# Two edits to the load order of a fused attention and feed-forward kernel: eight attention loads behind a feed-forward step, and one weight load cut in two

## The chip, the core and the metric

The kernel runs on one core of a Trainium2 chip. The core has a matrix engine (TensorE; PE in the profile, with PEld for its weight loads), VectorE (DVE), ScalarE (ACT), GpSimd (POOL) and a sync engine (SP), and 16 DMA engines that they share. Each engine works through its own list of instructions in order and waits on semaphores for the others. The metric is the device time of one execution in microseconds (us), and the median of several runs is compared.

## What is computed

Sliding-window causal attention over 8 sequences of 576 tokens with 8 heads of 64, then a gated feed-forward block (SwiGLU) over the 4608 tokens. Inputs are float32; the kernel works in bf16 on the chip and writes float32.

```python
scores = q @ k.T / 8
mask = (rel >= 0) & (rel < 64)          # rel = query position - key position
attn = softmax(where(mask, scores, -1e9))
x = (attn @ v) reshaped to [4608, 512]  # heads side by side
g = x @ w_gate                          # [512, 1536]
out = (silu(g) * (x @ w_val)) @ w_out   # [1536, 512]
```

## The kernel before, in words

**Tiles.** The 4608 tokens are 36 chunks of 128 (number n) and 9 groups of 512 (c). Chunk n belongs to group n // 4. For the attention a chunk needs its own keys and the last 64 of the chunk before, so the work for chunk n reads k and v of n - 1 and n. The 1536 columns of the feed-forward block are 12 slices of 128 (f).

**Steps.** `F(c, fs, lo, hi)` computes slices fs of group c for the tokens lo to hi of the group: 4 gate products per slice on PE into one PSUM bank, a tanh on ACT (tile sig), 4 value products into a second bank, then two operations on DVE (tiles uu and hT). Its products are recorded on line 918, and it keeps the last of them as `self.lastF`. `O`, `O2` and `O3` are the output products of 128 tokens (12 matmuls on line 962), their copy (to tile ost) and, for O and O3, the store. `S2(n)` is the scores of chunks n and n + 1 (PE lines 471 and 475), their exponentials on ACT (line 483) and a mask multiplication on DVE (line 497). `AVw(n)` is the weighted values of chunks n and n + 1 (PE line 620, chunk n first and then n + 1) and their division by the row sums on DVE. `B2(n)` does the scores of chunks n + 2 and n + 3 interleaved with the weighted values of n and n + 1. `X(n)` transposes the attention result xb of chunk n into xT, which F reads. Up to chunk 5 this is done on PE, and from chunk 6 on by a DMA transpose on SP's queue (line 808).

**Loads.** All loads of k, q, v and weights are DMAs issued by POOL, which casts float32 to bf16 on the way. They go out in the order of the program and share one software queue (q0 in the profile). Keys and queries of chunks 4 to 11 come in pairs of chunks through `load2` (tiles ks and qs, line 335) and are transposed on PE by `T64` (line 385). From chunk 12 on they come one chunk at a time through `load` (tiles kn and qn, line 325) and are transposed by DMA on SP (`Tkq`, `T`, line 370). SP's queue is in order: X(6), X(7), then the four transposes of chunks 12 and 13, then X(8), X(9), and so on. `load` and `load2` take a gate: a DMA with a gate is issued only after the operation named, and all that stands behind it on POOL waits with it.

**The order around the change.** It is written out by hand in `build`. In the opening, POOL issues k and q of chunks 2 and 3, v of chunks 0 to 3, the weights of slices 0 to 3 with four copies between them, the weights of slices 4 to 7, k and q of chunks 4 and 5, the weights 8 to 11, and so on up to `halves(4)` and `halves(5)`: two copies on POOL each, which put the halves of two value tiles side by side in tile vs (line 256). AVw(4) reads them, the first two for chunk 4 and the last two for chunk 5. Group 0's F steps run on PE meanwhile, with T64(2) between F(0, (6,)) and F(0, (7,)).

Then group 1 starts. Its first 256 tokens (chunks 4 and 5) are ready first, so F is done on the halves: F(1, fs, 0, 256) for the slices 0 to 11 two at a time, and then F(1, fs, 256, 512), which needs xT of chunks 6 and 7. From AVw(6) on the order is: AVw(6), X(6), X(7), T64(4), O(0, 1), F(1, (6, 7), 0, 256), F(1, (8, 9), 0, 256), S2(8), T64(5), the transposes of chunks 12 and 13, F(1, (10, 11), 0, 256), F(1, (0, 1), 256, 512), O2(0, 2), B2(8), X(8), X(9), F(1, (2, 3), 256, 512), a gated load of k and q of chunks 14 and 15, F(1, (4, 5), 256, 512), O2(0, 3) and B2(10). B2(10) is the first to read k and q of chunks 12 and 13 and v of chunks 10 and 11 (the tiles va 0 and 1).

**PSUM banks.** There are eight; each step takes the one that was used longest ago in the order of the program. F(1, (2, 3), 256, 512) takes the bank from which DVE has copied O2(0, 2), and the second scores of B2(8) take the bank of the value products of F(1, (0, 1), 256, 512), which DVE reads last.

**Semaphores of DMAs.** POOL's DMAs use 16 semaphores in turn, so each also waits for the one 16 before it.

Of the kernel before, what the change touches and what calls it, by code (L numbers as in the profile page):

```python
# [153 lines left out]
class _Kernel:  # L154
# [218 lines left out]
    def T64(self, st):  # L373
# [4 lines left out]
        def pe(e):  # L378
            for i, (x, src, _) in enumerate(loads):
                for a in range(8):  # L380
                    for u in range(2):
                        r = slice(64 * u, 64 * u + 64)
                        for p in range(2):
                            o = bx[u][0].bitcast(BF)[64 * p:64 * p + 64, 512 * i + 64 * a:512 * i + 64 * a + 64]
                            z = e.transpose(o, src[r, a, p, :], self.ident[r, r])  # L385
            return z
# [539 lines left out]
    def F(self, c, fs, lo=0, hi=512, mid=None, side=False):  # L926
        do = self.Fp(c, fs, lo, hi, side)
        for a in range(len(fs)):
            do("Wg", a)
        if mid:  # L930
            mid()
        do("tan", 0)
        for a in range(len(fs)):
            do("Wv", a)
        do("end", 0)

    def O(self, c, u, mid=None):
        io = (4 * c + u) % self.NO
        self.Omm(c, u, 0, 512, "act", [("ost", io), ("osth", io)], mid=mid)
        self.store(c, u)  # L940
# [56 lines left out]
    def loads(self):  # L997
        self.first_loads()
        self.init()
        self.init_mask()  # L1000
        done = self.init_nmask()
        self.init_va(2, 4)
        for i in range(4):
            self.zero(self.vs[i][:, :, 64:80], [("vs", i, 0), ("vs", i, 1)], 1.0)
        self.load2(1, done)
        for n in range(4):
            self.load(n, "v")
        self.W(0, 2)
        self.shift(0, 1, "pool")
        self.W(2, 4)  # L1010
        self.shift(2, 0, "pool")
        self.shift(2, 1, "pool")
        self.shift(3, 0, "pool")
        self.load_w("g", 4, 8)
        self.load_w("v", 4, 6)
        self.load_w("v", 6, 8)

    def early_loads(self):
        self.load2(2)
# [18 lines left out]

    def next_loads(self):
        self.load2(5)  # L1040
        for n in (12, 13):
            self.load(n, "kq")
        for n in (10, 11):
            self.load(n, "v")

    def loop_loads(self, n):
        for m in (n + 6, n + 7):
# [8 lines left out]
    def build(self):  # L1056
# [96 lines left out]
            ev("q", u, "act")  # L1153
        O(0, 1)
        F(1, (6, 7), 0, 256)
        F(1, (8, 9), 0, 256)
        self.init_kmask()
        self.S2(8)
# [34 lines left out]
        for c in range(2, NFC):  # L1193
            for u in range(4):
                n = 4 * c + u + 4
# [6 lines left out]
                v = u + 1 if c == 2 else u  # L1202
# [71 lines left out]
```

## Time and profile before

| What | us |
|---|---|
| Runs before | 326.47, 327.15, 329.30; median 327.15 |
| The profiled execution, whole | 327.38 |
| Its span in the profile | 325.6 |
| PE busy | 318.3 |
| DVE busy | 220.0 |
| ACT busy | 125.7 |
| POOL busy | 106.0 |

The span starts at the first instruction and ends at the last. All times in the rows below are microseconds from its start. The whole execution is 1.78 us longer than the span; that part lies around it. The granted clock of PE is 1.00 in this execution.

The profile also shows the DMA engines in 40 equal slices of 8.14 us each, as a share of all 16 that is busy, in tenths:

```profile
DMA  7999999969999989959999997999687312000012
```

From 8 to 65 us the slices stand at 9. Three queues share the engines:

```profile
q0 software_dynamic: 99504, 18.36, 69.6%
q1 hardware_dynamic: 42864, 10.89, 23.8%
q10 hardware_dynamic: 5472, 9.83, 8.8%
```

Each row is a queue with its packets, the megabytes written and the share of 16 engines' span. q0 holds the DMAs that POOL issues, q1 those of SP (the transposes, and the first loads), q10 those of ACT (the stores of the output).

A row of the timeline gives the start, the length, the engine, the line, the operation and its tiles, and in brackets how long the engine had been idle and what released it. "Landing" is the time from the issue of a DMA to its completion.

### The profile page before, as it was taken

What the parts mean: (1) busy time and instruction counts of PE and PEld (TensorE: products, weight loads), DVE (VectorE), ACT (ScalarE), POOL (GpSimd) and SP (SyncE); (2) the same over time, 40 slices, a digit from 0 to 9 for tenths busy, and PEclk for the clock granted to TensorE, in tenths of its full rate; (3) what the DMA queues carried; (4) which work ended last, traced back from release to release, by engine and by line L of the source; (5) the groups of instructions that cost most, each with busy time, mean ns of one, the idle gap of its engine ahead of it and who ended that gap; (6) DMA issues with size and microseconds to landing.
All of it is one profiled execution on the core that took longest, in us unless ns stands there. A gap on an engine that the chain in (4) does not pass through costs nothing.

```text
span 325.6 us, 8051 instructions
## 1 busy us (share of the span) xinstructions
PE 318.3 (98%) x3446; PEld 169.3 (52%) x3446; DVE 220.0 (68%) x408; ACT 125.7 (39%) x226; POOL 106.0 (33%) x137
## 2 busy tenths in 40 slices
PE   7999999799999999999999999999999999999996
PEld 5655677568544554545444454545454544444444
DVE  6788996679485966675858585858676767555510
ACT  3834565634332543333324242424242422322311
POOL 6999790041726051607060606151402000000000
DMA  7999999969999989959999997999687312000012
GB/s 188 178 199 188 200 183 188 143 93 139 153 165 153 133 86 142 162 117 142 132 104 125 141 151 73 139 131 158 84 102 106 74 34 64 34 32 32 34 64 97
DMA packets 147875, 39.59 MB, mean 122 GB/s; under 512 B 131328, under 2 KB 142848, under 8 KB 147840
## 3 DMA queue, kind: packets, MB, share of 16 engines
q0 software_dynamic: 99504, 18.36, 69.6%
q1 hardware_dynamic: 42864, 10.89, 23.8%
q10 hardware_dynamic: 5472, 9.83, 8.8%
q8 instruction: 27, 0.44, 0.6%
q14 instruction: 8, 0.07, 0.1%
HBM read 37.75 MB, written 9.44 MB: 145 GB/s over the span
## 4 chain that ended last, share of the span: by engine, by line
PE 91%; DMA 4%; POOL 2%; issue 1%; DVE 1%; ACT 1%
PE ps L918 55%; PE ps L962 29%; DMA Wv<-in_moe_w_val_dram 3%; PE ps L729 2%; DMA va<-in_v_dram 2%; PE ps L521 2%; PE ps L471 1%; PE ps L385 1%; POOL vs L256 1%; PE ps L475 0%; POOL va L325 0%; PE ps L620 0%; ACT xT L255 0%; POOL ks L335 0%; PE ps L552 0%
## 5 line engine op out<-in xcount | busy, mean ns | idle before, releaser
L918 PE MATMUL ps<-xT,Wg 128*128 128x512 bf16 (+1 forms) x496 | 111.2, 352 | 1.7 <-issue 1.7
L904 DVE SCALAR_TENSOR_TENSOR uu<-sig,ps 128x512 bf16<-128x512 bf16 x108 | 73.9, 684 | 56.0 <-ACT sig L899 55.6
L918 PE MATMUL ps<-xT,Wv 128*128 128x512 bf16 (+1 forms) x496 | 111.0, 352 | 0.3 <-DMA Wv<-in_moe_w_val_dram 0.3
L899 ACT ACTIVATE sig<-ps 128x512 bf16<-128x512 f32 x108 | 65.1, 602 | 89.4 <-PE ps L918 89.4
L962 PE MATMUL ps<-Wo,hT 128*128 128x512 bf16 (+1 forms) x444 | 98.7, 373 | 0.0
L906 DVE SCALAR_TENSOR_TENSOR hT<-uu,ps 128x512 bf16<-128x512 bf16 x108 | 74.2, 687 | 3.8
L918 PEld LDWEIGHTS ps<-xT,Wv 128*128 128x128 bf16 x496 | 48.3, 98 | 45.4 <-DVE uu L904 0.8
L918 PEld LDWEIGHTS ps<-xT,Wg 128*128 128x128 bf16 x496 | 46.7, 98 | 44.5 <-issue 2.1
L962 PEld LDWEIGHTS ps<-Wo,hT 128*128 128x128 bf16 x444 | 43.3, 98 | 49.0
L325 POOL DMA_DIRECT2D kn<-in_k_dram x27 | 23.0, 853 | 113.9 <-PE ps L918 113.9
L325 POOL DMA_DIRECT2D va<-in_v_dram x40 | 34.2, 878 | 24.9 <-PE ps L918 24.9
L255 ACT ACTIVATE ost<-ps 128x512 f32<-128x512 f32 (+1 forms) x22 | 12.9, 588 | 53.2 <-PE ps L962 53.2
L256 DVE COPY ost<-ps 128x512 f32<-128x512 f32 (+1 forms) x15 | 10.1, 674 | 30.6 <-PE ps L962 30.6
L531 ACT ACTIVATE pt<-ps 128x512 bf16<-128x512 f32 x36 | 18.6, 602 | 29.0 <-PE ps L521 29.0
L325 POOL DMA_DIRECT2D qn<-in_q_dram x27 | 23.1, 861 | 0.0
L483 ACT ACTIVATE pt<-ps 128x512 bf16<-128x512 f32 x28 | 14.5, 602 | 14.7 <-PE ps L475 14.7
L764 DVE TENSOR_TENSOR xb<-ps,rc 128x512 bf16<-128x512 f32 (+2 forms) x39 | 18.8, 509 | 0.5
L729 PE MATMUL ps<-va,pt 64*64 64x65 bf16 x800 | 12.3, 192 | 0.0
L497 DVE TENSOR_TENSOR pt<-pt,kmask 128x1024 bf16<-128x1024 bf16 x18 | 11.5, 682 | 0.0
L729 PEld LDWEIGHTS ps<-va,pt 64*64 64x64 bf16 x800 | 10.4, 107 | 0.0
L497 DVE TENSOR_TENSOR pt<-pt,mask 128x1024 bf16<-128x1024 bf16 x14 | 9.3, 689 | 1.2 <-ACT pt L483 1.1
L760 DVE RECIPROCAL rc<-ps 128x8 f32<-128x8 f32 (+2 forms) x39 | 5.7, 173 | 6.4 <-PE ps L729 6.4
(76 smaller groups left out, 142.2 us busy)
## 6 DMA issues: line engine op xcount, KB each, us to landing
out_dram<-ost ACTq DMA_DIRECT2D x35, 256.0 KB, 2.6
va<-in_v_dram POOLq DMA_DIRECT2D x32, 128.0 KB, 5.8
kn<-in_k_dram POOLq DMA_DIRECT2D x21, 128.0 KB, 4.4
qn<-in_q_dram POOLq DMA_DIRECT2D x21, 128.0 KB, 4.6
Wv<-in_moe_w_val_dram POOLq DMA_DIRECT2D x6, 256.0 KB, 9.2
Wo<-in_moe_w_out_dram POOLq DMA_DIRECT2D x4, 384.0 KB, 14.4
Wg<-in_moe_w_gate_dram POOLq DMA_DIRECT2D x4, 256.0 KB, 8.5
ks<-in_k_dram POOLq DMA_DIRECT2D x3, 256.0 KB, 10.8
```

The lines of the kernel that those rows point to most:

```text
L256: return self.g.op(eng, lambda e: e.tensor_copy(d, a), reads=reads, writes=writes, after=after)
L325: self.g.op("pool", lambda e, d=d, a=a: e.dma_start(d, a), writes=ks, dma=True, after=gate)
L483: g.op("act", lambda e, po=po, p=p: e.activation(po, sv[p], ACTF.Exp, scale=SCALE), reads=[bx[p][1]], writes=[pk[p]])
L497: self.g.op("dve", lambda e: e.tensor_tensor(pt, pt, m, ALU.mult), reads=pk + mk, writes=pk)
L531: g.op("act", lambda e, po=po, p=p: e.activation(po, sv[p], ACTF.Exp, scale=SCALE), reads=[bx[p][1]], writes=[pk[p]])
L729: x = e.matmul(o, ab[0], ab[1], start=first, stop=phase == 1, skip_group_check=True)
L764: g.op("dve", lambda e, av=av, hs=hs, w=w, rc=rc, xo=xo: e.tensor_tensor(xo[:, :, hs, :], av[:, :, :, 0:64], rc[:, :, hs].unsqueeze(3).to_ ...
L899: g.op("act", lambda e: e.activation(sig[:, 0:w], G[:, 0:w], ACTF.Tanh, scale=0.5), reads=[gk], writes=[("sig", i)])
L904: g.op("dve", lambda e: e.scalar_tensor_tensor(uu[:, 0:w], sig[:, 0:w], 1.0, G[:, 0:w], ALU.add, ALU.mult), reads=[("sig", i), gk], writes ...
L906: g.op("dve", lambda e: e.scalar_tensor_tensor(out, v3(uu), 0.5, v3(V), ALU.mult, ALU.mult), reads=[("uu", i), vk], writes=[("hT", ih, f, ...
L918: r = e.matmul(bank[:, a * n:a * n + n], W[:, kk, f * 128:f * 128 + 128], xT[:, kk, lo:hi], start=(kk == 0), stop=(kk == NK - 1))
L962: r = e.matmul(OB[:, 0:n], hT[:, f, 128 * u:128 * u + 128], self.Wo[:, f, lo:hi], start=(f == 0), stop=(f == NF - 1))
```

## The change

Two edits:

1. The weights of slices 4 to 7 were loaded as one DMA of the gate weights for four slices and two DMAs of the value weights for two slices each. Now there are four DMAs of two slices each, in the order gate 4 and 5, value 4 and 5, gate 6 and 7, value 6 and 7. `W(a, b)` issues a gate load and a value load.
2. The loads of k and q of chunks 12 and 13 (six DMAs, since chunk 13 crosses from one sequence to the next) and of v of chunks 10 and 11 (two DMAs) stood right behind `load2(5)` with no gate. Now they stand behind F(1, (6, 7), 0, 256) and wait for its last product.

```diff
@@ loads @@
-        self.load_w("g", 4, 8)
-        self.load_w("v", 4, 6)
-        self.load_w("v", 6, 8)
+        self.W(4, 6)
+        self.W(6, 8)
@@ next_loads @@
     def next_loads(self):
         self.load2(5)
+
+    def after_loads(self):
         for n in (12, 13):
-            self.load(n, "kq")
+            self.load(n, "kq", self.lastF)
         for n in (10, 11):
-            self.load(n, "v")
+            self.load(n, "v", self.lastF)
@@ build @@
         F(1, (6, 7), 0, 256)
+        self.after_loads()
         F(1, (8, 9), 0, 256)
```

The instructions of PE, DVE, ACT and SP keep their order; POOL has one DMA more.

## The prediction

> **What bounds the kernel now.** I read the busy shares first, then PE's waits, then the timeline around each wait.
>
> ```profile
> PE 318.3 (98%) x3446; PEld 169.3 (52%) x3446; DVE 220.0 (68%) x408; ACT 125.7 (39%) x226; POOL 106.0 (33%) x137
> ...
> PE ps L918 <- issue: 1.7, 1, 1.7
> ```
>
> PE is busy for 98% of the span, so the load order can act only through PE's few stalls. This wait is the longest. It is called "issue": the profile shows no releaser. The timeline around it, and around a wait on a weight DMA:
>
> ```profile
> 21.71 1.03 PE L918 MATMUL ps<-xT,Wv 128*128 128x512 bf16 x4
> 22.57 1.03 PE L918 MATMUL ps<-xT,Wg 128*128 128x512 bf16 x4
> 23.93 1.02 PE L918 MATMUL ps<-xT,Wv 128*128 128x512 bf16 x4 [0.34 <-DMA Wv<-in_moe_w_val_dram]
> ...
> 57.72 1.05 PE L918 MATMUL ps<-xT,Wg 128*128 128x256 bf16 x8
> 58.60 1.04 PE L918 MATMUL ps<-xT,Wv 128*128 128x256 bf16 x8
> 61.34 1.03 PE L918 MATMUL ps<-xT,Wg 128*128 128x256 bf16 x8 [1.69 <-issue]
> ```
>
> A step of four such products takes 0.86 from start to start (22.57 - 21.71), one of eight halves 0.88. So PE was ready at 23.43 and began at 23.93 (0.50 lost), and was ready at 59.48 and began at 61.34 (1.86 lost). The last row is F(1, (0, 1), 256, 512), the first reader of X(6) and X(7).
>
> ```profile
> 51.40 2.64 SPq L808 DMA_TRANSPOSE xT<-xb  x2
> ...
> xT<-xb SPq DMA_TRANSPOSE x1, 8.5
> ...
> q0 software_dynamic: 4000, 0.57, 187.7%
> q10 hardware_dynamic: 144, 0.26, 17.8%
> ...
> xT<-xb SPq DMA_TRANSPOSE x1, 2.4
> ```
>
> SP issues X(6) and X(7) at 51.40 and about 52.7. X(7) took 8.5 to land, at 61.2: that is the stall, 0.1 before PE's start. The two queue rows are for the stretch 51.4 to 55.8: the load queue q0 moved 4000 packets, and the transposes' queue q1 has no row. The last line is X(8), issued at 68.02 with no load on the way: 2.4.
>
> **The loads leave the transposes' way.**
>
> ```profile
> 41.41 0.70 POOL L335 DMA_DIRECT2D qs<-in_q_dram  x1
> 42.10 0.89 POOL L325 DMA_DIRECT2D kn<-in_k_dram  x1
> ...
> 45.19 1.41 POOL L325 DMA_DIRECT2D qn<-in_q_dram  x2
> 46.53 1.85 POOL L325 DMA_DIRECT2D va<-in_v_dram  x2
> ...
> qs<-in_q_dram POOLq DMA_DIRECT2D x1, 256.0 KB, 12.6
> ...
> va<-in_v_dram POOLq DMA_DIRECT2D x1, 128.0 KB, 16.0
> ```
>
> The last load ahead of the eight moved ones landed at 41.41 + 12.6 = 54.0, and v of chunk 10 at 46.53 + 16.0 = 62.5. With the eight gone, q0 is empty at 54.0. X(6) and X(7) then land between 52.7 + 2.4 = 55.1 and, if they start only at 54.0 and one issue apart, 54.0 + 1.3 + 2.4 = 57.7. Both are before 59.48, so the stall goes whole: -1.86. Its floor is zero (the first rival).
>
> **The wait that is added.**
>
> ```profile
> 53.84 1.04 PE L918 MATMUL ps<-xT,Wv 128*128 128x256 bf16 x8
> ...
> 67.84 1.04 PE L918 MATMUL ps<-xT,Wv 128*128 128x256 bf16 x8
> ...
> 69.18 0.88 POOL L325 DMA_DIRECT2D kn<-in_k_dram  x1 [20.79 <-PE ps L918]
> ```
>
> From the gate's last product (68.88) to the gated DMA (69.18) are 0.30, so the new gate opens POOL at 53.84 + 1.04 + 0.30 = 55.2. Behind it stand only the eight loads, until the load that goes at 69.18 anyway. They take POOL 6.3 (42.10 to 48.38), so it is free at 61.5. The first transfers start after 55.2, and X(6) and X(7) have 55.1 to 57.7. Who waits for the loads is SP, for the four transposes of chunks 12 and 13, and then B2(10) on PE.
>
> ```profile
> 73.71 0.24 PE L471 MATMUL ps<-qT,kT 64*64 64x128 bf16 x2
> ...
> 117.45 0.88 POOL L325 DMA_DIRECT2D kn<-in_k_dram  x1 [12.47 <-PE ps L918]
> ...
> 127.74 1.19 SPq L370 DMA_TRANSPOSE qT<-qn  x1
> ...
> qT<-qn SPq DMA_TRANSPOSE x1, 2.4
> ```
>
> The first row is the last reader in B2(10), the scores of chunk 13: 1.86 earlier is 71.85. The other three are the nearest case: at 117.45 POOL issues the same eight loads (k, q, a split k, a split q, two v), and the last transpose behind them goes at 127.74 and lands 2.4 later, 12.7 after the first issue. From 55.2 that is 67.9, and 69.2 with one transpose more (1.3). So 2.6 are left, and it costs nothing. The last v, issued 5.4 after the first load (47.45 after 42.10), at 60.6, has some 11. The far end, the third rival, is the landing that these loads had in the crowded queue.
>
> X(8) and X(9), behind these transposes on SP, are read first by F(2, (0,)), near 80.
>
> **The weight DMA in two.**
>
> ```profile
> 14.45 0.74 POOL L345 DMA_DIRECT2D Wg<-in_moe_w_gate_dram  x1
> 15.18 1.50 POOL L345 DMA_DIRECT2D Wv<-in_moe_w_val_dram  x2
> ...
> 15.18 8.62 DMA Wv<-in_moe_w_val_dram
> ...
> Wv<-in_moe_w_val_dram POOLq DMA_DIRECT2D x1, 256.0 KB, 9.2
> ```
>
> The value weights of slices 4 and 5 landed at 23.80, and those of 6 and 7, issued at about 15.92, at 25.1: 1.3 for 256 KB on the queue. Half of the gate load now goes behind the former, so they land near 22.5, and the 0.50 at 23.93 goes. The gate weights of 6 and 7 land near 23.8 and are wanted at 23.43 + 3 x 0.86 = 26.0. But POOL issues one DMA more, 0.74, and in front of these copies:
>
> ```profile
> 12.56 1.94 POOL L256 COPY vs<-va 64x512 bf16<-64x512 bf16 x3 [0.57 <-DMA va<-in_v_dram]
> 31.13 3.47 POOL L256 COPY vs<-va 64x512 bf16<-64x512 bf16 x4
> ...
> 14.64 0.19 PE L644 MATMUL ps<-vs,pt 128*64 128x65 bf16 x1 [0.55 <-POOL vs L256]
> 35.32 0.19 PE L620 MATMUL ps<-vs,pt 128*64 128x65 bf16 x1
> ```
>
> POOL shows no idle time between 12.56 and 31.13, so the four copies end at 31.13 + 3.47 + 0.74 = 35.34. PE follows a copy by 0.14 (14.50 to 14.64): chunk 5 of AVw(4) can start at 35.48. It started at 35.32, and with 0.50 won it would want 34.82. So this stage ends at +0.16: the gain is taken back by POOL's issue. Ends: -0.50 if the copies come earlier (the second rival), and +0.35 with an issue of 0.93 (half the va row of 46.53). I take +0.16, as POOL runs without a gap.
>
> On the queue the halves are the same bytes. The next that could be late is T64(2):
>
> ```profile
> 18.05 1.36 POOL L335 DMA_DIRECT2D qs<-in_q_dram  x2
> 28.34 0.45 PE L385 MATMUL ps<-ident,ks 64*64 64x64 bf16 x32
> ...
> qs<-in_q_dram POOLq DMA_DIRECT2D x1, 192.0 KB, 8.5
> ```
>
> Its last load lands at 18.75 + 8.5 = 27.25 and is wanted at 28.34 - 0.50 = 27.84: with a lag of 0.14, 0.45 of cover.
>
> **What is late next** after the stall is DVE.
>
> ```profile
> 63.76 0.69 DVE L906 SCALAR_TENSOR_TENSOR hT<-uu,ps 128x512 bf16<-128x512 bf16 x1
> 65.87 0.69 DVE L256 COPY ost<-ps 128x512 f32<-128x512 f32 x1 [1.43 <-PE ps L962]
> ...
> 66.96 1.05 PE L918 MATMUL ps<-xT,Wg 128*128 128x256 bf16 x8
> ```
>
> DVE ends its work of the F steps at 64.45 in either case. The copy of O2(0, 2) then ends at 65.14 at the earliest, and the step that takes its bank wants to start at 66.96 - 1.86 = 65.10; with the lag, 65.28. I take +0.2, between 0 and +0.4.
>
> **Sum:** -1.86 + 0.16 + 0.2 = -1.5; ends -2.4 and -1.1. The profiled execution's 327.38 (span 325.6 and 1.78 around it) becomes 325.9. It lies 0.23 over the median of 327.15, which becomes 325.6.
>
> **The rivals.**
>
> 1. *The stall stays.* The transposes are slow by themselves next to any traffic, and X(7) lands at 61.2 still. For it: the output stores (q10, 144 packets) share the engines too. Against it: 2.4 for X(8), and no q1 packet while q0 moved 4000. Only the +0.16 is left: 327.3. The Trainium skill, DMA: Bandwidth & Descriptors, section Queues, rings and completion order, says that a DMA engine goes round its queues packet by packet, so a full load queue alone shouldn't hold the transposes for 4.4. The 4000 packets against none speak against that rule in this stretch; by it the sum would be this rival's.
> 2. *POOL's extra issue bites nothing.* Then the 0.50 stays as well: -1.86 - 0.50 + 0.2, 325.0.
> 3. *The moved loads come too late,* the one on the other side. The second half of q of chunk 13 is issued 3.8 after the first load (45.89 after 42.10), at 59.0. If it lands as slowly as v of chunk 10 did (16.0) and its transpose as slowly as X(7) (8.5), B2(10) waits from 71.85 to 83.5, and the kernel takes 337. It decides from 71.85 on, is slower than before from 73.4, and by over 1% from 76.7. Against it: those 16.0 were queueing behind earlier loads, and now q0 is empty at the gate.
> 4. *The extra DMA holds the queue* for as long as a whole 256 KB does, 1.3: T64(2) starts at 27.25 + 1.3 + 0.14 = 28.69, 0.35 late, and the sum is -1.3. The same page, section Anatomy of one DMA, gives each DMA a fixed 2.0 beside its bytes; held in a row that would make T64(2) 1.05 late and the sum -0.6, an estimate from that page. The two value loads landed 1.3 apart with bytes and all, so the trace doesn't bear 2.0 in a row out.
>
> That the wait isn't there is no rival: the gate is an explicit dependency of each of the eight DMAs.
>
> **How the numbers follow.** The forecast has 0.70, the rivals 0.10, 0.08, 0.08 and 0.04. The runs before spread by 2.8, so I reach from 324.4 (the second rival less 0.6) to 327.9 (the first and 0.6); what is left out is the third rival and scatter. One per cent is 3.3, about what a measurement of this kernel can tell from no change. All cases but the third stay within it. Faster by more would take over twice the stall, and no row offers that: 0.05. Slower by more is most of the third rival: 0.07. Within: 0.88.
>
> **What would show it.** Right: no wait of PE at F(1, (0, 1), 256, 512), X(7) landing in under 5; gated loads starting near 55; no PE wait on Wv near 23, and one on POOL's vs copies at 35; B2(10) with no wait. Wrong: a transpose of chunk 13 landing after 71.8, PE waiting on a load or on SP there, or X(7) still taking 8.

## The result and the profile after

| | before | changed |
|---|---|---|
| Median of 14 runs each | 326.68 | 325.44 |
| Lowest to highest | 326.17 to 329.30 | 324.88 to 325.94 |
| The profiled execution | 327.38 (span 325.6) | 325.72 (span 324.0) |

The ratio of the changed kernel to the one before is 0.9949, with a 95% interval of 0.9931 to 0.9967: about 0.5% faster, which is within 1%. Below, a ratio is always to the kernel before on the same chip.

The busy shares and PE's waits in the changed kernel's profile:

```profile
PE 314.4 (97%) x3411; PEld 169.3 (52%) x3446; DVE 218.6 (67%) x408; ACT 125.6 (39%) x226; POOL 106.5 (33%) x138
...
PE ps L918 <- issue: 2.2, 14, 0.2
PE ps L918 <- DMA Wv<-in_moe_w_val_dram: 0.9, 1, 0.9
```

The 2.2 of "issue" is no stall. It is 14 pieces of at most 0.2, and 3411 of 3446 matmuls have a record here: a missing record leaves a hole of about that size in the timeline. The wait of 1.7 in one piece is gone. This is the stretch where it was, in the timeline of PE:

```profile
57.96 1.05 PE L918 MATMUL ps<-xT,Wg 128*128 128x256 bf16 x8
58.85 1.04 PE L918 MATMUL ps<-xT,Wv 128*128 128x256 bf16 x8
59.72 1.04 PE L918 MATMUL ps<-xT,Wg 128*128 128x256 bf16 x8
```

The third row is F(1, (0, 1), 256, 512). It follows its neighbour after 0.87, where 2.74 lay between them before (58.60 to 61.34). The gain of this place is the difference, 1.87. The transposes that it reads, and the queues from their issue at 51.64 to 56.04:

```profile
51.64 2.76 SPq L808 DMA_TRANSPOSE xT<-xb  x2
...
xT<-xb SPq DMA_TRANSPOSE x1, 3.3
xT<-xb SPq DMA_TRANSPOSE x1, 3.5
...
q1 hardware_dynamic: 1088, 0.26, 36.2%
q10 hardware_dynamic: 257, 0.47, 28.4%
q0 software_dynamic: 65, 0.06, 7.7%
```

X(6) and X(7) land after 3.3 and 3.5, where X(7) took 8.5. The queue of the loads (q0) moved 65 packets in these 4.4, where it had moved 4000, and the queue of the transposes (q1) 1088, where it had none. (The share in such a row adds up the times of all packets; they overlap, so it can pass 100%.) The gate and what hangs on it:

```profile
55.42 0.88 POOL L325 DMA_DIRECT2D kn<-in_k_dram  x1 [12.97 <-PE ps L918]
...
64.93 1.19 SPq L370 DMA_TRANSPOSE qT<-qn  x1
...
qT<-qn SPq DMA_TRANSPOSE x1, 4.9
...
72.19 0.24 PE L471 MATMUL ps<-qT,kT 64*64 64x128 bf16 x2
```

POOL waits 13.0 and starts the eight loads at 55.42. The last of the four transposes lands at 64.93 + 4.9 = 69.8; its reader, the scores of chunk 13 in B2(10), starts at 72.19, without a wait.

In the opening, the execution after was the slower one:

```profile
17.22 1.05 PE L918 MATMUL ps<-xT,Wv 128*128 128x256 bf16 x8 [0.94 <-DMA Wv<-in_moe_w_val_dram]
...
24.17 1.03 PE L918 MATMUL ps<-xT,Wv 128*128 128x512 bf16 x4
...
28.58 0.45 PE L385 MATMUL ps<-ident,ks 64*64 64x64 bf16 x32
...
31.52 3.31 POOL L256 COPY vs<-va 64x512 bf16<-64x512 bf16 x4
```

PE waited 0.94 at 17.22 for the value weights of slices 0 and 1, which are issued ahead of anything that the change touches. It did not wait at 24.17 for those of slice 4. So it came to T64(2) at 28.58, 0.24 later than before, and to chunk 5 of AVw(4) after POOL's copies had ended (34.83), without a wait for them. Which of these waits an execution has, the experiments had to tell.

### The profile page after: what moved, and what is told of

Its sections match the earlier page's. It is cut to its first block, busy times and chain, and to the rows that moved or that the text cites. A ratio compares the mean times of both kernels' runs of the same rounds, so it can differ in the third digit from the quotient of the medians.

```text
span 324.0 us, 8018 instructions
## 1 busy us (share of the span) xinstructions
PE 314.4 (97%) x3411; PEld 169.3 (52%) x3446; DVE 218.6 (67%) x408; ACT 125.6 (39%) x226; POOL 106.5 (33%) x138
## 4 chain that ended last, share of the span: by engine, by line
PE 91%; DMA 2%; POOL 2%; issue 1%; DVE 1%; ACT 1%; ACTq 0%
PE ps L918 56%; PE ps L962 29%; DMA Wv<-in_moe_w_val_dram 2%; PE ps L729 2%; PE ps L521 2%; POOL va L325 1%; PE ps L471 1%; PE ps L475 0%; ACT xT L255 0%; PE ps L385 0%; ACT sig L899 0%; POOL ks L335 0%; PE ps L552 0%; POOL qs L335 0%; POOL Wg L345 0%
## 5 line engine op out<-in xcount | busy, mean ns | idle before, releaser
L918 PE MATMUL ps<-xT,Wg 128*128 128x512 bf16 (+1 forms) x481 | 107.9, 351 | 2.3 <-issue 2.2
L962 PE MATMUL ps<-Wo,hT 128*128 128x512 bf16 (+1 forms) x436 | 97.4, 373 | 0.5 <-DVE hT L906 0.2
```

What stands on the lines that cost most here:

```text
L918: r = e.matmul(bank[:, a * n:a * n + n], W[:, kk, f * 128:f * 128 + 128], xT[:, kk, lo:hi], start=(kk == 0), stop=(kk == NK - 1))
L962: r = e.matmul(OB[:, 0:n], hT[:, f, 128 * u:128 * u + 128], self.Wo[:, f, lo:hi], start=(f == 0), stop=(f == NF - 1))
```

## The experiments

There were eleven runs. The first four take the change apart.

**Only the gate.** The weights are loaded as before:

```diff
-        self.W(4, 6)
-        self.W(6, 8)
+        self.load_w("g", 4, 8)
+        self.load_w("v", 4, 6)
+        self.load_w("v", 6, 8)
```

> Only the gate; the weights of slices 4 to 7 load as before. If the stall ahead of F(1, (0, 1), 256, 512) was the whole gain, that stall (1.86) is gone, PE still waits near 23.9 for the value weights of slice 4 in those executions where they land late (0.50), and the kernel takes 1.6 to 1.9 us less than before (ratio 0.994 to 0.995). If the weight split brought the gain, the ratio is 1.00 and X(7) still takes about 8 to land.

Measured: median 325.08, ratio 0.9954 (0.9936 to 0.9972). The profile has no stall ahead of F(1, (0, 1), 256, 512), and no wait for weights either. The gate alone brings the gain.

**Only the weight load in two.** The kernel before with `W(4, 6)` and `W(6, 8)`, and nothing gated.

> Only the weight load in two; the eight attention loads are not gated. My steps: the wait for the value weights of slice 4 is gone, POOL issues one DMA more ahead of its four copies, and the stall at X(7) stays at about 1.9: between 0.4 us faster and 0.2 slower than before (ratio 0.999 to 1.001). If the extra DMA held the load queue, T64(2) would start late by 0.35 or more and the kernel would be 0.4 to 1 us slower.

Measured: median 327.09, ratio 1.0009 (0.9998 to 1.0020): 0.3 on the slow side, and not told apart from nothing. The stall is there, though shorter in this execution:

```profile
58.37 1.04 PE L918 MATMUL ps<-xT,Wv 128*128 128x256 bf16 x8
60.32 0.93 PE L918 MATMUL ps<-xT,Wg 128*128 128x256 bf16 x7 [0.91 <-issue]
```

With the 0.87 of a step, PE was ready at 59.24 and lost 1.08. It did not wait near 23, but it waited 0.59 at 16.64 for the value weights of slices 0 and 1, as in the changed kernel.

**The four copies earlier.** In the changed kernel POOL's copies are put ahead of two loads:

```diff
-        self.load(6, "v")
-        self.load(7, "v")
         self.halves(4, "pool")
         self.halves(5, "pool")
+        self.load(6, "v")
+        self.load(7, "v")
```

> The changed kernel with POOL's four copies (halves of chunks 4 and 5) ahead of the loads of v of chunks 6 and 7, so that the copies end about 1.8 us earlier. If the copies held chunk 5 of AVw(4) as the prediction's sum had it, this is 0.2 to 0.5 us faster than the changed kernel (ratio to before 0.9935 to 0.994). If they end before PE asks for them, as in the trace of the changed kernel (34.83 against 35.56), nothing changes (0.9945 to 0.9955).

Measured: median 325.04, ratio 0.9944 (0.9932 to 0.9956). The difference to the changed kernel's 0.9949 is smaller than either interval, so the time settles nothing. Nor did the edit do all that its text expected:

```profile
30.87 3.34 POOL L256 COPY vs<-va 64x512 bf16<-64x512 bf16 x4 [1.09 <-DMA va<-in_v_dram]
```

POOL waited 1.09 for a load of v, and the copies ended at 34.21, 0.6 ahead of the changed kernel's 34.83 and not 1.8. What the extra DMA costs is read from all the traces together, below.

**The gate 4.8 later.** In the changed kernel:

```diff
         F(1, (6, 7), 0, 256)
-        self.after_loads()
         F(1, (8, 9), 0, 256)
...
-        for n in (12, 13):
-            self.Tkq(n)
         F(1, (10, 11), 0, 256)
+        self.after_loads()
+        for n in (12, 13):
+            self.Tkq(n)
```

> The changed kernel with the eight loads and the four transposes of chunks 12 and 13 behind F(1, (10, 11), 0, 256) instead of F(1, (6, 7), 0, 256): the gate opens 4.8 us later, near 60.2. The last transpose landed at 69.8 and is wanted at 72.2, so 2.4 are spare. Theory: it lands at 74.6, PE waits about 2.4 in B2(10), and the kernel is 2.4 us slower than the changed one and 0.8 slower than before (ratio 1.002). Rival: with POOL and the queue empty the loads and transposes run faster later, nothing waits, and it takes as long as the changed kernel (0.995). Second rival: they collide with the next loads and the wait is 5 or more (1.01 and up).

Measured: median 331.92, ratio 1.0153 (1.0140 to 1.0167). The second rival of that text came true: 6.5 slower than the changed kernel, not 2.4. The rows of POOL, SP and PE:

```profile
59.43 0.88 POOL L325 DMA_DIRECT2D kn<-in_k_dram  x1 [17.72 <-PE ps L918]
66.91 0.88 POOL L325 DMA_DIRECT2D kn<-in_k_dram  x1 [1.24 <-PE ps L918]
...
68.91 1.19 SPq L370 DMA_TRANSPOSE qT<-qn  x1
...
qT<-qn SPq DMA_TRANSPOSE x1, 7.5
...
72.70 0.24 PE L471 MATMUL ps<-qT,kT 64*64 64x128 bf16 x2 [1.75 <-issue]
76.50 0.31 PE L471 MATMUL ps<-qT,kT 64*64 64x128 bf16 x2 [2.92 <-DMA qT<-qn]
...
77.56 1.89 PE L918 MATMUL ps<-xT,Wg 128*128 128x256 bf16 x8
79.24 1.19 PE L918 MATMUL ps<-xT,Wv 128*128 128x256 bf16 x8
80.27 1.04 PE L918 MATMUL ps<-xT,Wg 128*128 128x256 bf16 x8
```

This execution was 0.75 ahead of the changed kernel's at T64(4), so the gate at 59.43 is 4.76 later by PE's steps. The last transpose goes out at 68.91, after the issue of the loads of chunks 14 and 15 has begun at 66.91. It takes 7.5, lands at 76.4, and PE goes on at 76.50. The collision that the change removes at X(6) and X(7) now hits the transposes of chunks 12 and 13: from 68.91 to 76.41, q0 moves 5102 packets.

With the 0.75 taken off, the scores of chunk 13 start 5.06 later than in the changed kernel (76.50 against 72.19). Another 1.35 comes behind them: from there to the third F row PE takes 3.77 (76.50 to 80.27), and 2.42 in the changed kernel (72.19 to 74.61). The matmuls are slower, because the granted clock of PE fell. It is 1.00 up to 76, 0.50 from 77 to 79, and 1.00 again from 80 on, so the gate products of the first F step take 1.68 instead of 0.88. All four runs of this kernel have a mean granted clock of 0.989 to 0.995. In the 40 slices of the profile's page (8.24 us each, in tenths of full speed, 9 for 90% and more) it is the 7:

```profile
PEclk9999999997999999999999999999999999999999
```

The stall of 1.9 in the kernel before left the clock at 1.00. So a wait of PE can cost more than its own length.

The next four ask where the margin ends, how many loads it takes, and what belongs to one execution only.

**The gate one step later:** `self.after_loads()` behind F(1, (8, 9), 0, 256).

> The changed kernel with the eight loads one step later, behind F(1, (8, 9), 0, 256): the gate opens 1.75 later. In the run with the gate 4.8 later the transposes of chunks 12 and 13 took 7.5 to 7.9 because they ran into the loads of chunks 14 and 15, and PE waited in B2(10). Theory: the cost is a collision and begins once the last transpose goes out within about 2 us of those loads' first transfers (they are issued near 67.5 and move from 69 on). Here the last transpose goes out near 66.7, lands near 71.6 if it takes 4.9 and at 74.4 if 7.7, and is wanted at 72.2: no wait to 2.2, ratio 0.995 to 1.001. Rival, a fixed chain: it lands 1.75 later than 69.8, 0.6 ahead of its reader, and the ratio is 0.995.

Measured: median 325.75, ratio 0.9965 (0.9945 to 0.9986). The last transpose goes out at 65.27, ahead of the next loads, takes 5.2, lands at 70.5, and its reader starts at 71.75 with no wait. So 1.3 are left of 2.4. The gate opened at 56.71, against 55.42 in the changed kernel; this execution was 0.46 ahead at T64(4), so by PE's steps it is 1.75 later. The 0.3 by which the median is slower is within the intervals. Theory and rival meet here (no wait, 0.995), so this run does not tell them apart. Its profile has one gap of 0.58 on PE at 75.35 in the middle of a step, where no semaphore is waited for; what it is stays open.

**Only k and q of chunks 12 and 13 gated,** and **only v of chunks 10 and 11 gated.** The other loads stand in `next_loads` as before.

> The changed kernel with only k and q of chunks 12 and 13 behind the gate; v of chunks 10 and 11 loads at once, as before. 2048 packets of the load queue (1.8 us at the 1165 per us of the trace) then stand ahead of X(6) and X(7). Theory (the transposes wait for what is queued ahead of them): X(6) starts moving near 53.5 to 54.5 instead of 52.5, X(7) lands near 57.5, 2 ahead of its reader, no stall, ratio 0.995 as the changed kernel. If any queued load at all delayed them as the eight did, X(7) lands at 61 and the ratio is 1.000.

> The changed kernel with only v of chunks 10 and 11 behind the gate; k and q of chunks 12 and 13 load at once, as before: 4096 packets (3.5 us) stand ahead of X(6) and X(7). Theory: X(6) starts moving near 55.5 to 56 as in the kernel before, but nothing is behind it that shares the engines, so X(7) lands near 58.5 to 59.5, at about the time its reader wants it: stall 0 to 0.3, ratio 0.995 to 0.996. If the engines went round the queues packet by packet from the moment of the issue, X(6) would move from 52.5 on, in step with q0.

Measured: 325.34, ratio 0.9945 (0.9927 to 0.9964), with k and q gated; 325.88, ratio 0.9972 (0.9952 to 0.9992), with v gated. The landing times of X(6) and then X(7), first with two loads ahead of them (k and q gated), then with six (v gated):

```profile
xT<-xb SPq DMA_TRANSPOSE x1, 5.2
xT<-xb SPq DMA_TRANSPOSE x1, 4.3
```

```profile
xT<-xb SPq DMA_TRANSPOSE x1, 7.0
xT<-xb SPq DMA_TRANSPOSE x1, 6.4
...
q0 software_dynamic: 2925, 0.49, 167.9%
q1 hardware_dynamic: 7, 0.00, 0.2%
```

The queue rows are for 51.14 to 54.9 of the kernel with v gated: 2925 packets of q0 and 7 of q1, so the two queues did not move evenly there. Over all the profiles with these two transposes, the first packet on q1 after the issue of X(6) and the two landings are:

| Loads ahead | Profiles | First q1 packet after | X(6) lands after | X(7) lands after |
|---|---|---|---|---|
| none | 7 | 1.26 to 1.32 | 3.25 to 4.33 | 3.32 to 4.65 |
| two (v) | 1 | 2.13 | 5.23 | 4.33 |
| six (k and q) | 1 | 3.67 | 7.03 | 6.37 |
| all eight | 3 | 4.46 or 4.47 | 7.21 to 7.35 | 7.73 to 8.50 |

The start of the transposes grows with the loads ahead of them and repeats within 0.06. The landings scatter more: X(7) behind two loads is within the range of none. Two things stay open. The profile shows when packets move, not when those of a transpose stand ready, so what holds them back is not told. And where k and q load early, the four transposes of chunks 12 and 13 go out early too (from 54.86 before, 54.56 with v gated, 58.96 in the changed kernel). They stand behind X(7) on SP; whether they slow its last part was not separated.

Neither kernel has a stall at F(1, (0, 1), 256, 512). The one with v gated is the slower in the median, but the intervals overlap. Its stretch from T64(4) to O2(0, 3) is 0.5 longer than the changed kernel's; 0.38 of that is a gap inside B2(8) whose cause the profile does not name.

**The kernel before, once more.**

> The kernel before, unchanged, for a second profile: whether the waits near 16 to 24 on the weight DMAs and the stall of 1.9 at F(1, (0, 1), 256, 512) belong to the kernel or to one execution. Expected: the stall at 59 to 61 is there again within 0.5; PE's wait at 23.9 on the value weights of slice 4 (0.5) may be absent, as in the run with only the gate.

Measured: 326.57 in its one run. The stall is there, and no wait near 23:

```profile
58.28 1.04 PE L918 MATMUL ps<-xT,Wv 128*128 128x256 bf16 x8
60.54 0.71 PE L918 MATMUL ps<-xT,Wg 128*128 128x256 bf16 x5 [1.22 <-issue]
```

PE lost 60.54 - 58.28 - 0.87 = 1.39. So with all eight loads ahead the stall took 1.86, 1.39 and, in the kernel with only the weights split, 1.08. Its size belongs to the execution, its presence to the kernel.

**X(6) and X(7) without DMAs.** The kernel before, with the two transposes made on PE and copied by ACT:

```diff
-        X(6)
-        X(7)
         ev = self.T64(4)
...
         F(1, (6, 7), 0, 256)
+        X(6, "act")
+        X(7, "act")
         F(1, (8, 9), 0, 256)
```

> The kernel before, all loads as before, but xT of chunks 6 and 7 made by transposes on PE and copies on ACT (behind F(1, (6, 7), 0, 256)) instead of by SP's DMAs. If the stall ahead of F(1, (0, 1), 256, 512) is the late landing of X(7) and nothing else, it goes although the eight loads are where they were; PE pays about 0.5 for the eight transposes and ACT 1.2 for two copies in a stretch where it is close to full: 0.3 to 1.2 us faster than before (ratio 0.996 to 0.999). If the stall has another cause that the loads bring with them, it stays and the kernel is 0.5 slower (1.0015).

Measured: median 325.64, ratio 0.9966 (0.9946 to 0.9986). PE's rows:

```profile
54.38 0.61 PE L821 MATMUL ps<-ident,xb 128*128 128x128 bf16 x8
...
58.78 1.04 PE L918 MATMUL ps<-xT,Wv 128*128 128x256 bf16 x8
59.65 1.04 PE L918 MATMUL ps<-xT,Wg 128*128 128x256 bf16 x8
```

All eight loads are where they were, and the stall is gone: the steps follow each other after 0.87. So the stall was the wait for these two DMA transposes, and no other effect of the loads on PE.

**The changed kernel again,** and **only the gate, with the copies earlier.**

> The changed kernel again, beside the next one: ratio 0.995 to before. From T64(2) to T64(3) PE took 11.33 without a wait for POOL's copies and 11.43 to 11.76 with one in the runs with the weights in two; here one of the two, by whether the first weights landed late in this execution.

> Only the gate (weights as before), and POOL's four copies ahead of the loads of v of chunks 6 and 7. Theory: without the extra DMA the copies end 0.7 sooner already and never hold AVw(4), so moving them does nothing more: as with only the gate, 0.1 to 0.4 us faster than the changed kernel (ratio to before 0.9935 to 0.995). If the weight split is worth its 0.5, this is slower than the changed kernel by up to that.

Measured: 325.42, ratio 0.9951 (0.9936 to 0.9966), and 325.01, ratio 0.9943 (0.9920 to 0.9967). The second is the lower in the median by 0.4, and the intervals overlap; nothing shows that the split is worth its 0.5. The copies of POOL and chunk 5 of AVw(4) in the changed kernel's second execution:

```profile
31.30 3.29 POOL L256 COPY vs<-va 64x512 bf16<-64x512 bf16 x4
...
34.73 0.19 PE L620 MATMUL ps<-vs,pt 128*64 128x65 bf16 x1 [0.31 <-POOL vs L256]
```

The copies end at 34.59, and PE starts 0.14 later after a wait of 0.31. The same row with only the gate, and then with only the weights split:

```profile
30.52 3.29 POOL L256 COPY vs<-va 64x512 bf16<-64x512 bf16 x4
```

```profile
31.26 3.29 POOL L256 COPY vs<-va 64x512 bf16<-64x512 bf16 x4
```

One DMA more puts the end from 33.81 to 34.55. These are two executions, but the others agree: from the end of POOL's earlier copies (near 14) to the end of these it is 19.90 to 20.10 in the four profiles with one DMA less, and 20.61 to 20.67 in the seven with the split and the copies in their old place. What PE loses by it is read from T64(2) to T64(3), because no other wait of over 0.2 shows between them:

| Kernel | T64(2) starts | to T64(3) |
|---|---|---|
| before | 28.34 | 11.33 |
| before, again | 27.95 | 11.33 |
| only the gate | 27.25 | 11.34 |
| only the gate, copies earlier | 27.57 | 11.34 |
| X(6), X(7) on PE | 27.74 | 11.34 |
| changed, copies earlier | 27.95 | 11.33 |
| changed | 28.58 | 11.33 |
| changed, again | 27.28 | 11.83 |
| gate 4.8 later | 27.40 | 11.76 |
| k and q gated | 27.51 | 11.75 |
| v gated | 27.98 | 11.43 |
| gate one step later | 27.99 | 11.47 |
| only the weights split | 28.00 | 11.34 |

The first six have one DMA less ahead of the copies, or the copies earlier, and all take 11.33 or 11.34. The last seven have the split, and take up to 0.5 more, most of it where PE is early.

## Why the prediction was right

**The stall.** The step held in cause and in size: -1.86 was forecast, and 1.87 lies between the two profiled executions. X(7) landed at 56.6, where 55.1 to 57.7 was forecast. The gate alone brings the gain, and the stall goes with the loads in place once X(6) and X(7) are no DMAs. What the prediction could not see is that 1.86 was one draw: other executions with the same eight loads ahead lost 1.39 and 1.08. The medians of all runs differ by 1.24, and the ratio's interval is 1.1 to 2.3 us.

**The first rival** (the transposes are slow by themselves) falls with the first packets of q1, 1.3, 2.1, 3.7 and 4.5 after the issue with none, two, six and eight loads ahead. With it goes the sum by the rule of the Trainium skill, DMA: Bandwidth & Descriptors, section Queues, rings and completion order, that an engine goes round its queues packet by packet. The traces do not show such a round where the load queue is full: 4000 packets against none before, 2925 against 7 with v gated. Whether the rule itself fails there is not shown, since it is about queues with work at the engine, and the profile does not say when the transposes' packets got there. Later both queues move: from 56 to 59 in the kernel before, 1405 packets of q0 and 1041 of q1.

**The gate's margin.** Forecast: opens at 55.2, last transpose at 69.2, 2.6 ahead of its reader. Measured: 55.42, 69.8 and 2.4. The row at 117.45, the same eight loads in the same order, was the right one to read this from.

**The third rival** (the moved loads come too late) did not happen, but it was close in a way that its text missed. It put the danger in loads that land slowly. The run with the gate 4.8 later shows it in the next gated loads, which collide with the transposes: 6.5 us for 4.8 of delay, some 1.35 of it at a lower clock of PE, which no rival had. The first 1.75 of delay cost nothing that the intervals can tell from zero.

**The weight load in two.** Half of this term's working failed, and +0.16 came close by luck. POOL's extra DMA does move the copies by 0.74 (33.81 to 34.55), and PE does start chunk 5 of AVw(4) 0.14 after their end where it has to wait for them. But the 0.50 that this was to take back was a wait of the one profiled execution. In the four other profiles with the old weight order PE did not wait there. So the split is no gain that is paid back; it is a cost of 0 to 0.5 against a wait that was seen once in five. The runs cannot tell it from nothing (1.0009, from 0.9998 to 1.0020). One of the prediction's signs, a wait for POOL's copies at 35, is missing in the changed kernel's first profile; three of the seven with the split and the copies in their old place show it (0.31, 0.24 and 0.23).

Another wait the prediction did not have. PE waits for the value weights of slices 0 and 1 in four of the eight profiles with the split (0.94, 0.59, 0.38 and 0.31), and by no more than 0.2 in the five without it. These loads are issued near 9.1, some 5 ahead of the first one that differs. Whether the split has a part in it stays open.

**The fourth rival** (the extra DMA holds the queue) did not happen. The last load that T64(2) needs landed at 19.07 + 8.14 = 27.21 in the changed kernel, against 27.17 before, and no profile shows T64(2) waiting for it.

**DVE after the stall.** Forecast +0.2, between 0 and +0.4. From the value products of F(1, (10, 11), 0, 256) to F(1, (2, 3), 256, 512) PE took 8.36 before and 6.59 after (58.85 to 65.44): 1.77 less, where the stall alone was 1.86. The cost is 0.09, at the low end. With the stall taken off, the three executions that have it took 6.49 or 6.50 there; of the ten without it, six took 6.59 to 6.61, two 6.49 and 6.50, and two 6.75 and 7.07. So about 0.1 is lost in most of them, but no row names DVE's copy as what PE waited for, and the cause that the prediction gave is not shown.

**The sum.** -1.5 was forecast for the profiled execution, and it fell by 1.66 (327.38 to 325.72). It is made up otherwise than forecast: +0.24 in the opening, where a wait of 0.94 came and one of 0.50 went, -1.87 at the stall and +0.1 behind it are -1.52 (65.44 against 66.96); where the last 0.14 lies was not followed. The median came to 325.44 against the 325.6 forecast, and that is partly luck too: the three runs known before had their median 0.47 above that of all 14 (327.15 against 326.68), which made up for a gain of 1.24 instead of 1.5.

## What to carry to other kernels

Look for a short transfer that PE waits for and ask what was queued on the same DMA engines just before its issue. Loads that are not needed yet belong behind it, and the gate has to leave room up to the next burst of loads too, because what is moved can run into that one. A wait can also cost more than it lasts, as the lower clock behind the late gate shows. A wait that one profile shows beside a DMA may be that execution's alone: a second profile of the kernel before costs one run and tells which terms of the sum can be trusted.

## What the runs showed of the hardware

- Two DMA transposes issued while loads of k, q and v from POOL were queued did not share the engines with them from their issue on. With eight loads ahead, their queue moved nothing for the first 4.46 us, in which the load queue moved about 4000 packets; with none ahead, its first packet came after 1.27. The second transpose landed after 8.5 instead of 3.5.
- After two waits of PE close together (1.75 and 2.92 in the rows, with the gate 4.8 later) the granted clock was 0.50 from 77 to 79, and the eight gate products of an F step took 1.68 instead of 0.88. After the stall of 1.9 in the kernel before it stayed at 1.00.
- The landing of the first weights differs between executions: the value weights of slices 0 and 1 landed 6.9 after their issue in the profile before and 8.1 in the one after, and PE waited 0.94 for them in the second. Over the 13 profiles T64(2) starts anywhere from 27.25 to 28.58, a spread as large as the median gain of this change (1.24).
